# Linear attention and a per-sequence expert on one core: attention output made transposed, its mean square by a matmul with ones, rstd by ln and exp

## The chip, the cores and the metric

The program runs on one core of a Trainium2 chip. The metric is the device time of one execution in microseconds (us); lower is better. The engines are named as the profile names them: PE is TensorE (PEld its weight loads), DVE is VectorE, ACT is ScalarE, POOL is GpSimd and SP is SyncE, which here only issues output transfers.

## The reference

Eight batches, eight heads, 576 positions, head size 64. Attention has no softmax: each head forms a 64 by 64 matrix from k and v, multiplies q by it, and normalises every head's output row by its root mean square. Each batch is then one token for a mixture of experts: the mean over its positions chooses one of eight experts, and the whole batch goes through that expert's two matrices.

```python
def _attn_ref(q, k, v, g_norm):
    kv = np.einsum('bhsd,bhse->bhde', k, v)
    out = np.einsum('bhsd,bhde->bhse', q, kv)
    rms = np.sqrt(np.mean(out * out, axis=-1, keepdims=True) + 1e-06)
    return (out / rms * g_norm).astype(np.float32)
# x: heads side by side, (8, 576, 512)
def _moe_ref(x, w_gate, w1, w2):
    logits = x.mean(axis=1) @ w_gate               # (8 batches, 8 experts)
    e_idx = np.argmax(logits, axis=1)
    ...                                            # gate_w: softmax of the logits at e_idx
    for e in range(E):
        mask = e_idx == e
        h = np.maximum(x[mask] @ w1[e], 0.0)       # 512 -> 1024
        out[mask] = gate_w[mask, None, None] * (h @ w2[e])   # 1024 -> 512
```

All inputs and the output are float32 in HBM. Both kernels turn q, k, v and the expert weights into float16 on the way in, which only POOL's queue does, so all of these loads are issued by POOL.

## The kernel before

A batch is worked in two parts. **Attention** (`emit_attention`) goes over five row blocks (128, 128, 128, 128, 64 positions). q, k, v arrive with positions on partitions: 128 partitions with 4 rows each per head, and a last piece of 64 partitions with one row (L98 and L100: six transfers a batch). ACT rearranges q (L106, L107). PE forms the 64 by 64 matrices head by head, 40 small matmuls a batch (L126), and DVE casts each pair into a block-diagonal tile `kv_dbuf` (L131, L132). For each row block PE transposes q (L211), DVE copies it out (L214), PE makes the output `po` with positions on partitions (L229), ACT squares it (L236), DVE sums the squares per head (L237), ACT copies the output (L240). The reciprocal root is an integer first guess with two Newton steps on DVE (L183 to L196), applied on DVE (L200). One batch later PE transposes the normalised float32 output back (L218) and ACT writes it as `xT` (L222), since the expert needs features on partitions.

**The gate** (`emit_pooled_front`, `emit_pooled_back`) sums the row blocks on DVE (L268 to L271), sums over partitions on POOL with a partition all-reduce (L273), transposes that on PE, multiplies by the gate weights, does a second all-reduce on POOL (L288), then finds the maximum, the index and the softmax value. POOL reads the index (L306) and issues the loads of the chosen expert, `w1f` and `w2f` (L310, L311).

**The expert** of batch b-2 is laid between the steps of batch b's attention: eight units of eight 288-column matmuls into two PSUM tiles `pha`, `phb` (L139, L141) with two Relus on ACT (L143, L144), and five units of eight 512-column matmuls (L152), scaled on DVE (L155) and written by SP (L158). The framework's scheduler orders the instructions on each engine. An engine works its own list strictly in order, so an instruction that waits holds back all that stand behind it, transfers on POOL's list included.

## Time and profile before

| | before |
|---|---|
| median of 3 runs | 307.0 us (305.02 to 308.94) |
| span of the profiled execution | 304.0 us |
| PE busy | 234.4 us (77%) |
| DVE busy | 163.1 us (54%) |
| ACT busy | 128.5 us (42%) |
| POOL busy | 81.9 us (27%) |
| moved by DMA | 40.68 MB, of which 30.94 MB loads by POOL's queue (counted as float16) |
| read from HBM | 61.88 MB |

The profiled execution is one run with its own time, its span; the median of the timed runs lies 3.0 us above it. Busy PE time is counted to the modelled end of each matmul, and matmuls overlap, so the distance between the starts of two matmuls, not the busy time of one, says how fast they follow each other. In the window view the columns are the stretch in us, its length, then for each engine busy us and instructions, then the TensorE clock granted (1.00 is 2.4 GHz, 0.50 is 1.2 GHz), then the DMA share and GB/s.

### The profile page before, as it was taken

To read this page: it belongs to the slowest core of one execution; us is meant where nothing else is said; L and a number is where in the kernel's file an instruction comes from. 1 tells how busy PE (TensorE), PEld (TensorE's weight loads), DVE (VectorE), ACT (ScalarE), POOL (GpSimd) and SP (SyncE) were. 2 spreads that over 40 slices of the span, in tenths; PEclk is the share of its full clock that TensorE was granted. 3 is DMA by queue.
4 is the path that set the end of the run, shared out by engine and by line. 5 is a ranking of instruction groups with operands and counts; after the bars stand their busy time and mean duration, and the time that the engine had idled before them with its cause. 6 is when DMAs were issued, how large, how long until landed. Compare 5 with 4: busy or idle time off the path is not lost.

```text
span 304.0 us, 4581 instructions
## 1 busy us (share of the span) xinstructions
PE 234.4 (77%) x1680; PEld 153.3 (50%) x1680; DVE 163.1 (54%) x532; ACT 128.5 (42%) x273; POOL 81.9 (27%) x88
## 2 busy tenths in 40 slices
PE   0028578716899519997999599989987988599994
PEld 0027456515564317745764377457545744464651
DVE  3004894794038704487749653976495478412122
ACT  1006663704483044942791159136613842440520
POOL 0755415048236123620402040204020420420000
PEclk9999655556799956999999689999997999989999
DMA  0599999079999999999308910595089229839712
GB/s 2 66 174 192 190 192 121 0 82 198 200 185 174 250 201 189 116 166 246 76 0 153 243 38 3 100 233 100 3 151 241 41 20 227 187 59 186 189 59 97
DMA packets 56104, 40.68 MB, mean 134 GB/s; under 512 B 14610, under 2 KB 47378, under 8 KB 56082
## 3 DMA queue, kind: packets, MB, share of 16 engines
q0 software_dynamic: 50176, 30.94, 73.7%
q1 hardware_dynamic: 5906, 9.46, 9.3%
q8 instruction: 13, 0.21, 0.3%
q14 instruction: 9, 0.07, 0.1%
HBM read 61.88 MB, written 9.44 MB: 235 GB/s over the span
## 4 chain that ended last, share of the span: by engine, by line
PE 42%; DMA 35%; DVE 8%; issue 6%; POOL 4%; ACT 3%; POOLq 1%; DVEq 0%; ACTq 0%
DMA w1f<-in_moe_w_dram 13%; PE phb L141 10%; PE pha L139 10%; DMA qb<-in_q_dram 9%; PE pmo L152 8%; PE pkv L126 5%; DMA out_dram<-ot 5%; PE pxt L218 4%; DMA kt<-in_k_dram 4%; DMA vt<-in_v_dram 4%; PE po L229 2%; PE pqt L211 2%; DVE ot L155 1%; POOL zbc L288 1%; POOL pbc L273 1%
## 5 line engine op out<-in xcount | busy, mean ns | idle before, releaser
L152 PE MATMUL pmo<-w2f,hT 128*128 128x512 f16 (+1 forms) x320 | 74.1, 380 | 0.0
L139 PE MATMUL pha<-xT,w1f 128*128 128x288 f16 x256 | 60.1, 303 | 11.9 <-DMA w1f<-in_moe_w_dram 11.6
L141 PE MATMUL phb<-xT,w1f 128*128 128x288 f16 x256 | 59.9, 301 | 1.2 <-ACT hT L143 0.6
L126 PE MATMUL pkv<-vt,kt 128*64 128x64 f16 (+1 forms) x320 | 31.4, 222 | 28.9 <-DMA vt<-in_v_dram 22.7
L273 POOL PARTITION_ALL_REDUCE pbc<-acc x8 | 25.8, 3231 | 87.6 <-DVE acc L271 81.1
L155 DVE TENSOR_SCALAR ot<-pmo,gates_all 128x512 f32<-128x512 f32 (+1 forms) x40 | 29.7, 746 | 34.2 <-PE pmo L152 18.6
L152 PEld LDWEIGHTS <-hT 128*128 128x128 f16 (+1 forms) x320 | 30.3, 100 | 34.5 <-issue 3.4
L143 ACT ACTIVATE hT<-pha 128x288 f16<-128x288 f32 x64 | 27.4, 428 | 42.0 <-PE pha L139 41.8
L126 PEld LDWEIGHTS <-kt 128*64 128x64 f16 (+1 forms) x320 | 23.9, 124 | 38.9 <-issue 17.4
L222 ACT ACTIVATE xT<-pxt,gcol 128x512 f16<-128x512 f32 (+1 forms) x35 | 22.7, 648 | 42.2 <-PE pxt L218 42.1
L139 PEld LDWEIGHTS <-w1f 128*128 128x128 f16 x256 | 26.1, 103 | 21.3 <-DMA w1f<-in_moe_w_dram 12.7
L237 DVE TENSOR_REDUCE ms<-sq_sb 128x8 f32<-128x512 f16 (+1 forms) x40 | 27.2, 681 | 14.4 <-ACT sq_sb L236 13.9
L218 PE MATMUL pxt<-ident,x_sb 128*128 128x128 f32 (+1 forms) x140 | 26.8, 319 | 9.8 <-ACT xT L222 8.1
L236 ACT ACTIVATE sq_sb<-po 128x512 f16<-128x512 f32 (+1 forms) x40 | 24.4, 610 | 22.0 <-PE po L229 21.6
L141 PEld LDWEIGHTS <-w1f 128*128 128x128 f16 x256 | 26.0, 102 | 10.9 <-issue 4.2
L106 ACT COPY qt<-qb 128x2048 f16<-128x2048 f16 x8 | 15.3, 1909 | 36.0 <-DMA qb<-in_q_dram 36.0
L131 DVE CAST kv_dbuf<-pkv 64x64 f16<-64x64 f32 x32 | 6.9, 215 | 42.1 <-PE pkv L126 42.0
L144 ACT ACTIVATE hT<-phb 128x288 f16<-128x288 f32 x64 | 27.0, 421 | 2.9 <-PE phb L141 2.0
L214 DVE COPY qT_sb<-pqt 128x512 f16<-128x512 f16 (+1 forms) x40 | 15.6, 394 | 19.7 <-PE pqt L211 19.2
L200 DVE TENSOR_TENSOR x_sb<-x_sb,y 128x512 f32<-128x512 f32 (+1 forms) x40 | 25.4, 682 | 0.2
L218 PEld LDWEIGHTS pxt<-ident,x_sb 128*128 128x128 f32 (+1 forms) x140 | 18.4, 168 | 12.6 <-ACT xT L222 9.1
L240 ACT COPY x_sb<-po 128x512 f32<-128x512 f32 (+1 forms) x40 | 23.8, 596 | 0.0
(57 smaller groups left out, 225.6 us busy)
## 6 DMA issues: line engine op xcount, KB each, us to landing
w1f<-in_moe_w_dram POOLq DMA_DIRECT2D x8, 1024.0 KB, 9.7
w2f<-in_moe_w_dram POOLq DMA_DIRECT2D x8, 1024.0 KB, 16.4
out_dram<-ot SPq DMA_DIRECT2D x32, 256.0 KB, 6.7
kt<-in_k_dram POOLq DMA_DIRECT2D x8, 512.0 KB, 11.6
vt<-in_v_dram POOLq DMA_DIRECT2D x8, 512.0 KB, 11.9
qb<-in_q_dram POOLq DMA_DIRECT2D x8, 512.0 KB, 12.1
out_dram<-ot SPq DMA_DIRECT2D x8, 128.0 KB, 5.3
kt<-in_k_dram POOLq DMA_DIRECT2D x8, 64.0 KB, 11.1
```

What stands on the lines that cost most here:

```text
L126: nc.tensor.matmul(pkv[o64:o64 + 64, pr, o64:o64 + 64], kt[0:js, h, j, :], vt[0:js, h, j, :], start=(j == 0), stop=(j == NJ - 1),)
L139: nc.tensor.matmul(pha, w1f[:, c, fb * P:(fb + 1) * P], xT[:, b, c, 0:288], start=(c == 0), stop=(c == 3))
L141: nc.tensor.matmul(phb, w1f[:, c, fb * P:(fb + 1) * P], xT[:, b, c, 288:576], start=(c == 0), stop=(c == 3))
L143: nc.scalar.activation(hT[:, fb, 0:288], pha, AF.Relu)
L144: nc.scalar.activation(hT[:, fb, 288:576], phb, AF.Relu)
L152: nc.tensor.matmul(pmo[0:js], hT[:, fc, soff:soff + js], w2f[:, fc, :], start=(fc == 0), stop=(fc == 7))
L155: nc.vector.tensor_scalar(out=ot[0:js], in0=pmo[0:js], scalar1=gates_all[0:js, b:b + 1], scalar2=None, op0=ALU.mult)
L200: nc.vector.tensor_tensor(x_sb[0:js, j, :].rearrange("p (h e) -> p h e", h=H), x_sb[0:js, j, :].rearrange("p (h e) -> p h e", h=H), y0[0:j ...
L218: nc.tensor.transpose(pxt[:, c, 0:js], xo_sb[0:js, i, c * P:(c + 1) * P], ident[0:js, 0:js])
L236: nc.scalar.activation(sq_sb[0:js], po[0:js], AF.Square)
L237: nc.vector.reduce_sum(ms[0:js, j, :], sq_sb[0:js].rearrange("p (h e) -> p h e", h=H), axis=AX.X)
L273: nc.gpsimd.partition_all_reduce(pbc, acc, P, ReduceOp.add)
```

## The change

The change rewrites the whole kernel around another layout:

- **Loads.** A head's 576 positions are loaded as 96 partitions with 6 rows each: one transfer for each of k, v, q of a batch instead of two, 768 instead of 1536 pieces. Batch 0 is split in two halves of four heads. Three pool buffers for the expert weights instead of two.
- **Relayout.** DVE rearranges q and k (`s_re`, L98); ACT did it for q before.
- **Attention transposed.** PE transposes q per head pair (L107), forms two heads' matrices in one 128-column matmul (L118, 24 a batch instead of 40), and makes the output with features on partitions (L129), 288 columns at a time. The transposition back (L218 before) is gone.
- **Mean square.** ACT squares (L132); a matmul with a block-diagonal matrix of 1/64 (L145) sums over the 64 features of each head and spreads the sum over them; ACT takes Ln and Exp with scale -0.5 (L148, L150). One DVE instruction multiplies by the root and by g, writes `xT` in float16 and sums over the positions on the way (L151).
- **Gate.** Four small float32 matmuls on that sum (L159) give the logits on all partitions; the two all-reduces on POOL are gone.
- **Expert.** Relu over 576 columns in one instruction (L214), the scaling over two blocks at once (L231). Rows of the output leave as pieces of 32, 64 or 96 partitions (L241, nine transfers a batch instead of five).
- **Order.** The order is that of the Python code, per engine. Batches 0 and 1 do their attention alone; then the expert of batch b carries the attention of batch b+2 between its 13 units. Two PSUM groups, `a` and `m`, of two double banks each.

```diff
+    for b in (0, 1):
+        for u in att_steps(b, ("a", "m")):
+            u()
+    for b in range(B):
+        mu = moe_units(b)                      # m_1 x8, m_2 x5
+        au = att_steps(b + 2, ("a",)) if b + 2 < B else []
+        first = 1
+        ai = 0
+        for i, u in enumerate(mu):
+            u()
+            want = 0 if i < first else -(-len(au) * (i - first + 1) // (len(mu) - first))
+            while ai < want:
+                au[ai]()
+                ai += 1
...
+    def s_re(b, hs):
+        for n, i in (("qr", 2), ("kr", 0)):
+            nc.vector.tensor_copy(s[n][0:R, :, hs, :],
+                                  kvq[b][i][0:R, hs].rearrange("p h j d -> p j h d"))
...
+    def s_m(b, c, tag):
+        for i in range(2):
+            nc.tensor.matmul(pm[:, i, 0:HS], ones, sq[:, i * HS:(i + 1) * HS],
+                             start=True, stop=True)
+        nc.scalar.activation(ln.rearrange("p (i n) -> p i n", i=2), pm[:, :, 0:HS],
+                             AF.Ln, bias=epsc)
+        nc.scalar.activation(ln, ln, AF.Exp, scale=-0.5)
+        nc.vector.scalar_tensor_tensor(out=s["xT"][:, c, :], in0=o, scalar=gcol, in1=ln,
+                                       op0=ALU.mult, op1=ALU.mult,
+                                       accum_out=s["pl"][:, c:c + 1])
...
+    def s_gate(b, tag):
+        for c in range(NP):
+            nc.tensor.matmul(pg, s["pl"][:, c:c + 1].to_broadcast([P, P]), wg[:, c, :],
+                             start=(c == 0), stop=(c == NP - 1))
...
+        ev = nc.gpsimd.value_load(ix[0:1, 0:1], min_val=0, max_val=E - 1)
...
+        nc.gpsimd.dma_start(w1, moe_w1[ds(ev, 1)].rearrange("o (c p) f -> p (o c) f", p=P))
+        nc.gpsimd.dma_start(w2, moe_w2[ds(ev, 1)].rearrange("o (c p) d -> p (o c) d", p=P))
+        if b + 2 < B:
+            load_qkv(b + 2, 1)
-        pbc = att.tile([P, D], F32, tag="pbc")
-        nc.gpsimd.partition_all_reduce(pbc, acc, P, ReduceOp.add)
...
-        nc.gpsimd.partition_all_reduce(zbc, zt, P, ReduceOp.add)
...
-                pxt = psT.tile([P, 4, P], F32, tag="t")
-                for c in range(4):
-                    nc.tensor.transpose(pxt[:, c, 0:js],
-                                        xo_sb[0:js, i, c * P:(c + 1) * P],
-                                        ident[0:js, 0:js])
```

**POOL's list at the start of the program.** `ident` is the identity matrix for the transposes, `kt`, `vt`, `qb` or `qt` are the loads of k, v, q. First before, then after:

```order
masks.py:197 MEMSET ident 128x128
masks.py:197 MEMSET ident_96 128x128
masks.py:199 ISA
masks.py:199 AFFINE_SELECT ident<-ident 128x128
masks.py:199 AFFINE_SELECT ident_96<-ident_96 128x128
L98 DMA kt<-in_k_dram 128x8x256
L100 DMA kt<-in_k_dram 64x8x64
L98 DMA vt<-in_v_dram 128x8x256
L100 DMA vt<-in_v_dram 64x8x64
```

```order
L64 DMA kt<-in_k_dram 96x4x384
L64 DMA vt<-in_v_dram 96x4x384
L64 DMA qt<-in_q_dram 96x4x384
L64 DMA kt<-in_k_dram 96x4x384
L64 DMA vt<-in_v_dram 96x4x384
L64 DMA qt<-in_q_dram 96x4x384
masks.py:197 MEMSET ident 128x128
masks.py:199 ISA
masks.py:199 AFFINE_SELECT ident<-ident 128x128
```

The six loads of batch 0 now stand ahead of the making of the identity.

**POOL's list around an expert load in the middle of the program** (before: batch 1's expert; `pbc` and `zbc` are the two all-reduces, `ix` the chosen index), first before, then after:

```order
L273 ISA pbc<-acc 128x512
L100 DMA vt<-in_v_dram 64x8x64
L98 DMA qb<-in_q_dram 128x8x256
L100 DMA qb<-in_q_dram 64x8x64
L98 DMA kt<-in_k_dram 128x8x256
L100 DMA kt<-in_k_dram 64x8x64
L98 DMA vt<-in_v_dram 128x8x256
L288 ISA zbc<-zt 128x32
L100 DMA vt<-in_v_dram 64x8x64
L306 TENSOR_LOAD ix_897
L306 ISA x2
L310 DMA w1f<-in_moe_w_dram 128x4x1024
```

```order
L172 TENSOR_LOAD ix
L172 ISA x2
L175 ISA
L175 DMA w_423<-in_moe_w_dram 128x4x1024
L176 ISA
L176 DMA w_424<-in_moe_w_dram 128x8x512
L64 DMA kt<-in_k_dram 96x8x384
L64 DMA vt<-in_v_dram 96x8x384
L64 DMA qt<-in_q_dram 96x8x384
```

The only instruction on POOL that waits for DVE's work is now the read of the index; five transfers stand right behind it, the expert of batch b first and then q, k, v of batch b+2.

**DVE's list after the change, from the end of one round to the start of the next** (`ot` is an expert's output, `lg` to `gates` the gate of batch b+2, then the relayout of batch b+3, whose q and k must have landed):

```order
L151 SCALAR_TENSOR_TENSOR xT,pl<-o,gcol,ln 128x576
L231 TENSOR_SCALAR ot<-ps_m,gates 64x512
L162 COPY lg<-ps_a 128x8
L165 MAX mx<-lg 128x8
L166 MAX_INDEX ix<-mx,lg 128x8
L167 TENSOR_SCALAR lg<-lg,mx 128x8
L171 RECIPROCAL gates<-gs 128x1
L98 COPY qr<-qt 96x3072
L98 COPY kr<-kt 96x3072
L109 COPY qT<-ps_a 128x576 x4
```

None of these stood so before: there the relayout was ACT's, and the gate lay in the middle of a later batch's attention.

## Rows read from the trace of the kernel before

**Rows 1.** Page: span, and PE's busy time, share and instructions.

```profile
span 304.0 us, 4581 instructions
PE 234.4 (77%) x1680; PEld 153.3 (50%) x1680; DVE 163.1 (54%) x532; ACT 128.5 (42%) x273; POOL 81.9 (27%) x88
```

**Rows 2.** Windows by stage: stretch, length, engines' busy us, granted clock, DMA share, GB/s.

```profile
52.00:62.00 10.00, 7.23 (x60) 5.42 (x58) 6.57 (x32) 6.75 (x11) 0.01 (x1) 0.50 0.01 2
192.20:221.00 28.80, 26.59 (x212) 16.92 (x211) 19.42 (x66) 13.64 (x32) 5.41 (x4) 1.00 0.58 115
221.00:247.40 26.40, 23.07 (x163) 15.37 (x163) 16.86 (x55) 13.42 (x32) 5.40 (x4) 0.94 0.64 125
```

**Rows 3.** Waits: engine, line, for whom, us in total, times, longest.

```profile
POOL pbc L273 <- DVE acc L271: 81.1, 7, 15.6
...
PE pkv L126 <- DMA vt<-in_v_dram: 22.7, 3, 19.8
```

**Rows 4.** Timeline of the start: start us, us, engine, line, operation, idle before.

```profile
9.17 0.54 POOL masks.py:199 TENSOR_SCALAR_AFFINE_SELECT ident<-ident 128x128 f32<-128x128 f32 x2 [7.97 <-issue]
9.66 1.20 POOL L98 DMA_DIRECT2D kt<-in_k_dram  x1
...
22.82 1.90 ACT L106 COPY qt<-qb 128x2048 f16<-128x2048 f16 x1 [20.68 <-DMA qb<-in_q_dram]
```

**Rows 5.** Windows while only q, k, v load, and while an expert loads and outputs leave.

```profile
30.00:40.00 10.00, 6.27 (x64) 4.76 (x62) 8.17 (x35) 5.97 (x11) 4.85 (x7) 0.66 1.58 192
193.50:209.00 15.50, 14.06 (x116) 8.96 (x114) 13.03 (x37) 5.51 (x12) 0.76 (x2) 1.00 1.04 200
```

**Rows 6.** Chain that ended last, at the lower clock: start us, us, what.

```profile
57.96 1.12 PE pkv L126 x10
```

**Rows 7.** Timeline of PE at the full clock (starts tell the pace).

```profile
204.36 0.84 PE L126 MATMUL pkv<-vt,kt 128*64 128x64 f16 x10
205.13 0.40 PE L211 MATMUL pqt<-ident,qt 128*128 128x128 f16 x4
205.37 0.61 PE L218 MATMUL pxt<-ident,x_sb 128*128 128x128 f32 x4
...
272.71 8.91 PE L152 MATMUL pmo<-w2f,hT 128*128 128x512 f16 x40
...
283.52 0.28 PE L139 MATMUL pha<-xT,w1f 128*128 128x288 f16 x1
283.64 0.29 PE L141 MATMUL phb<-xT,w1f 128*128 128x288 f16 x1
...
284.67 0.28 PE L139 MATMUL pha<-xT,w1f 128*128 128x288 f16 x1
```

**Rows 8.** Groups by form: line, engine, operation, shapes, count, busy us, mean ns, idle before.

```profile
L143 ACT ACTIVATE hT<-pha 128x288 f16<-128x288 f32 x64 | 27.4, 428 | 42.0 <-PE pha L139 41.8
...
L155 DVE TENSOR_SCALAR ot<-pmo,gates_all 128x512 f32<-128x512 f32 x32 | 23.7, 747 | 23.3 <-PE pmo L152 17.5 <-PE phb L141 4.4 <-DMA out_dram<-ot 1.2
...
L200 DVE TENSOR_TENSOR x_sb<-x_sb,y 128x512 f32<-128x512 f32 x32 | 19.9, 683 | 0.0
L236 ACT ACTIVATE sq_sb<-po 128x512 f16<-128x512 f32 x32 | 19.7, 615 | 8.5 <-PE po L229 8.0 <-DVE ms L237 0.4
...
L214 DVE COPY qT_sb<-pqt 128x512 f16<-128x512 f16 x32 | 13.3, 421 | 10.2 <-PE pqt L211 9.7
...
L304 PEld LDWEIGHTS pg<-gsum,ones_row 1*128 1x128 f32 x16 | 2.5, 198 | 11.5 <-issue 7.0 <-DVE gsum L302 2.4 <-PE pmo L152 1.9
...
L214 DVE COPY qT_sb<-pqt 128x256 f16<-128x256 f16 x8 | 2.3, 288 | 9.5 <-PE pqt L211 9.4
```

**Rows 9.** Timeline around an expert load, and at the end: start us, us, engine, line.

```profile
190.77 0.15 DVE L295 FIND_INDEX8 ix<-mx,lrow 1x8 uint32<-1x8 f32 x1
...
192.22 0.76 POOL L310 DMA_DIRECT2D w1f<-in_moe_w_dram  x1 [1.99 <-DVE ot L155]
...
299.61 0.74 DVE L155 TENSOR_SCALAR ot<-pmo,gates_all 64x512 f32<-64x512 f32 x1 [1.09 <-PE pmo L152]
```

More of the change, by code (lines that the diff above doesn't have):

```diff
@@ new lines, in m_1 @@
+    def m_1(b, fb):
+        s = st[b]
+        if fb == 0:
+            s["hT"] = hp.tile([P, 8, S], F16, tag="hT", name="hT")
+        w1 = s["w"][0]
+        ph = psum("m")
+        for c in range(4):
+            for i in range(2):
+                nc.tensor.matmul(ph[:, i, 0:HS], w1[:, c, fb * P:(fb + 1) * P],
+                                 s["xT"][:, c, i * HS:(i + 1) * HS],
+                                 start=(c == 0), stop=(c == 3))
+        nc.scalar.activation(s["hT"][:, fb, :].rearrange("p (i n) -> p i n", i=2),
+                             ph[:, :, 0:HS], AF.Relu)
@@ new lines, in moe_units @@
+    def moe_units(b):
+        return ([lambda f=f: m_1(b, f) for f in range(8)]
+                + [lambda t=t: m_2(b, t) for t in range(5)])
+    for b in (0, 1):
[12 more added lines that the diff above has]
+                ai += 1
```

418 lines of the change are left out of this document (143 added, 275 removed).

## Prediction

> **What bounds the kernel now.** The page's first part comes first: no engine is full, and PE is the busiest with 234.4 of 304.0 us [rows 1]. So the end is set by PE's work plus what PE waits for, and the windows by stage say where it waits. Early there is a stretch, 52 to 62 us, in which nothing loads (DMA share 0.01) and PE works at a granted clock of 0.50, its lower level of 1.2 GHz; late, from one expert load to the next, a round takes 26.4 to 28.8 us with PE busy 87 to 92% of it at 0.94 to 1.00 [rows 2]. The waits say why loads stop: POOL stood 81.1 us in front of its all-reduce for DVE's sum, and the loads of q, k, v stand behind it on the same list; PE waited 22.7 us for v [rows 3]. The start shows a third cost: 7.97 us in which POOL, making the identity, has issued no load. The first one goes at 9.66 us, and q of batch 0 has landed at 22.82 [rows 4].
>
> How fast loads can be is in two windows. With q, k, v alone 192 GB/s arrive (float16; HBM is read at twice that); with an expert and outputs 200 GB/s together over 15.5 us, which is about what the expert of one round and the outputs beside it need [rows 5]. One batch of q, k, v is 1.77 MB, 9.2 us at 192 GB/s; one expert 2.10 MB. A round of loads is then 15.5 + 9.2 = 24.7 us.
>
> **The parts of the change, and the sum.** I lay the new order out in time, because nearly every instruction moves. Matmul prices are distances between starts.
>
> *Start.* The six loads of batch 0 now go ahead of the identity. The first is issued at about 0.9 us, so the data have landed by 0.9 + (22.82 − 9.66) = 14.1 us. Six issues of some 0.9 us and then the 7.97 us gap put the identity, which the first transpose needs, at 14.8 us. If the gap belongs to POOL's first work of any kind, nothing is gained: bounds 14.8 and 22.8. I take 14.8, since the gap ends in the identity's making and not in a load.
>
> *Attention alone, twice.* Batches 0 and 1 run with nothing beside them, so latencies add. Relayout of q: one DVE copy of 3072 float16 per partition. The rows have no such copy inside SBUF; the nearest is the transposes' copy, 288 ns for 256 and 421 ns for 512, so 0.52 ns each and 1.75 us for 3072; a float32 product at 683 ns for 512 would give about 3.4 us [rows 8]. I take 1.75. Transposes and the k-v matmuls, 48 at the lower clock, 0.11 us each by ten in 1.12 [rows 6]: 5.3. Two casts of 256 columns from PSUM at about 0.45 each (747 ns is the price of 512): 0.9. First output matmuls: 0.7. Then ACT is the chain: 4 Square, 4 Ln, 4 Exp over 576 columns. 428 ns for 288 and 615 for 512 give 0.67; with waits 0.69: 8.3. The last DVE product: 0.75. The gate is four float32 matmuls; before, one float32 product is two passes with loads of 198 ns [rows 8], so eight passes, 1.5. Sum 19.1 us. For batch 0 the relayout is already over at 14.8, so its gate is through PE at 14.8 + 17.4 = 32.2; batch 1's follows after 1.2 us more of gate on DVE: 52.5. I write 52 us to the first expert matmul.
>
> *First round.* The expert of batch 0 is issued 1.45 us after its index was found, as at 190.77 and 192.22 [rows 9]: at 34.5 us. It and q, k, v of batch 2 are 3.87 MB, 20.2 us at 192 GB/s, landed at 56.5. Relayout: 58.3. PE has done its first two expert units (1.9 us each at the lower clock) by 56 and waits 2.3 us. With these units and the next ones at the lower clock the first round is 6 us longer than the rest.
>
> *A round.* PE at the full clock: 64 expert matmuls of 288 columns at 0.12 us (283.52 to 283.64) make 7.7. Before, a unit took 1.15 us instead of 0.96 (283.52 to 284.67), since `phb` waits for a Relu in a rotation of three tiles; now two double tiles rotate, and a Relu of 0.67 us ends within the next unit. Were the gap to stay, 9.2. 40 matmuls of 512 columns: 8.75 (8.91 less the last one's tail). 24 transposes at 0.06 (205.13 to 205.37): 1.45. 24 k-v matmuls at 0.077 (204.36 to 205.13): 1.85. 16 matmuls of output and mean square at 0.12: 1.95 [rows 7]. Gate 1.45. Together 23.15 us.
>
> To this come three waits in PE's own order. (1) The first transpose follows two expert units (1.9 us) after the gate, but DVE must first end the gate (1.7) and copy q (1.75): 1.5 us. What waits behind DVE's copies are the transposes' copies; the expert's PSUM copies come 12 us later. (2) The output matmuls stand right behind the k-v matmuls and wait for both casts: 1.25 us. (3) The gate waits for the last Ln, Exp and product, 2 × 0.69 + 0.75 + some 0.4 of latency, less the one expert unit of 1.73 us beside them: 0.8 us. Round: 23.15 + 3.55 = 26.7 us. DVE has some 18 us in it (two relayouts 3.5, ten copies and casts from PSUM of 0.45 to 0.85, four products of 0.85, output scaling 3.6, gate 1.5) and ACT 13.7 (eight Relus of 0.67 and the 8.3 above), so neither is the bound. The nine outputs on SP and five loads on POOL wait for nothing that PE then waits for.
>
> The loads of a round (24.7 us) are issued some 4.7 us after the round before it ended, and are wanted 30 us after: with 1.5 us of latency they land at 30.9. That is a tie, hidden as long as the rate holds, because q, k, v may queue behind the previous round's.
>
> *Sum.* 52 + 6 + 6 × 26.7 (160.2) + two experts without attention at 7.7 + 8.75 + 0.25 (33.4) + the end as before, 304.0 less the last matmul at some 299.5 (4.5) [rows 1, 9] = 256 us of span. The profiled execution's span was 304.0 us against a median of 307.0, so 3 us are added: **259 us**.
>
> A page's price for the relayout: the Trainium skill, "VectorE: DVE Perf Modes", section "The perf-mode tier table", gives a float16 copy within SBUF four elements a cycle (693 ns for 2048), by which, as an estimate, 3072 would take about 0.95 us and the sum would be some 6 us lower. No row of before shows such a copy.
>
> **A rule against the change.** Before, transfers over 128 partitions bring q, k, v at 192 GB/s [rows 5]; no row shows 96 partitions. If the rate went with the partitions, it would be 144 GB/s and a batch 12.3 us: a round of loads becomes 27.8 us, above PE's 26.7. In favour of the change, a piece is now 6 rows long instead of 4 or 1, and there are half as many. The Trainium skill, "DMA: Bandwidth & Descriptors", section "Rules for kernel authors", asks for 128 partitions and at least 1 MiB a transfer for the most bandwidth, and these have 96 and 0.56 MiB; its section on why a DMA increments its semaphore by 16 says that 96 partitions still use all 16 engines. The first would give the load-bound rival below, the second leaves the sum.
>
> **The rivals.**
> *Loads bound the rounds.* At 27.8 us plus some lost between gate and issue, 28 a round: +1.3 × 6, and +3 in the first round's wait, so 270 us. For it: the tie above. Against it: the DMA share is 1.04 to 1.58 only while loading, and nothing ahead of a load waits any more.
> *Everything a little shorter.* Relayout at under 1 us (−6) and ACT's chain in the lonely attentions overlapping better (16 us each, −6): 247 us.
> *Waits between engines are longer than counted.* Each round crosses from PE to ACT or DVE and back about ten times; 0.33 us more at each is 30 us a round: 259 + 6 × 3.3 + 3 = 282 us. Before, rounds of 26.4 to 28.8 us held more crossings and as much PE work [rows 2].
> *Slower: TensorE stays at its lower level.* If the waits in the rounds kept the clock at 0.50, the 23.15 us of matmuls would become 46: 52 + 6 + 6 × 49.7 + 66 + 4.5 + 3 = 430 us. It decides from where the rounds reach 36 us, that is with the lower clock for 40% of the matmul time: then 313 us. For it: between 52 and 62 us the clock was 0.50 with PE busy 72%. Against it: 0.94 with PE 87% busy [rows 2]; the new rounds have PE at 23.15 of 26.7 us, 87%.
> *The change doesn't do what it says.* Order and lists do stand as described; one table set covers Square, Ln, Exp and Relu in ACT's list, which holds a single table load. No time hangs on this.
>
> **How the numbers follow.** My forecast (251 to 267): 0.48. Shorter throughout (238 to 251): 0.20. Loads bound (267 to 274): 0.16. Longer waits (274 to 300): 0.08. Lower clock (over 313): 0.05; something between 300 and 313: 0.03. The range reaches from 240 to 282, which leaves some 0.04 below and 0.12 above. Faster by over 2% (about what a measurement of this kernel can tell from no change) is below 301 us: 0.91; same 0.03; slower 0.06.
>
> **What would show it.** The first load issued near 1 us and the first transpose near 15; the first expert matmul near 52; expert loads 26 to 28 us apart with PE over 80% busy at a clock near 1.00; q landing about when DVE asks for it; relayout copies near 1.75 us; no POOL wait but for the index. Wrong would be: rounds over 30 us, DVE waiting microseconds for q in every round (loads bound), or a granted clock of 0.50 in the rounds.

## Result and profile after

| | before | after |
|---|---|---|
| median of runs side by side | 306.7 us (305.0 to 308.9, 4 runs) | 247.9 us (246.8 to 251.0, 4 runs) |
| span of the profiled execution | 304.0 us | 245.2 us |

The ratio is 0.807 (95% interval 0.802 to 0.812). The forecast was 259 us, in a range of 240 to 282. The time lies inside the range, 11 us under the figure, in the case called "everything a little shorter".

The page of the kernel after, first part (busy us, share of the span, instructions) and, from the second, the granted clock in 40 slices, in tenths:

```profile
span 245.2 us, 3595 instructions
PE 195.4 (80%) x1408; PEld 128.3 (52%) x1408; DVE 117.7 (48%) x240; ACT 107.9 (44%) x177; POOL 37.8 (15%) x49
...
PEclk9999755555999999988999999999999999999999
```

PE has 39 us less work than in [rows 1] and is still the busiest. Its idle time fell from 69.6 to 49.8 us. The lower clock (digits 5 and 7, some 25 to 60 us) lies in the stretch in which two batches do their attention with nothing beside them, and in the first round; by the pace of the matmuls it begins earlier (last section).

The expert loads on POOL's list cut both programs into three stretches. First two rows of the timeline of before, then of after (start us, us, engine, line, operation, idle before):

```profile
67.66 0.75 POOL L310 DMA_DIRECT2D w1f<-in_moe_w_dram  x1 [2.73 <-DVE tl L194]
...
269.31 0.76 POOL L310 DMA_DIRECT2D w1f<-in_moe_w_dram  x1 [1.98 <-PE pha L139]
```

```profile
1.44 0.81 POOL L64 DMA_DIRECT2D kt<-in_k_dram  x1 [0.87 <-POOLq L277]
...
5.84 0.29 POOL masks.py:199 TENSOR_SCALAR_AFFINE_SELECT ident<-ident 128x128 f16<-128x128 f16 x1
...
32.49 1.31 POOL L175 DMA_DIRECT2D w<-in_moe_w_dram  x1 [23.94 <-DVE gates L171]
...
209.12 0.75 POOL L175 DMA_DIRECT2D w<-in_moe_w_dram  x1 [22.03 <-PE ps_m L211]
```

Up to the first expert load: 67.66 against 32.49, 35.2 us gained. From the first to the last: 201.65 against 176.63, 25.0 us gained over seven loads. From the last to the end: 34.7 against 36.1, 1.4 us lost. Together 58.8, the whole difference of the spans. So three fifths of the gain are in the start, up to the issue of the first expert's load.

One round of after, by the windows from the first expert matmul of a batch to that of the next (columns as in [rows 2]): the first round, three of the five that follow it, and the last two experts, which have no attention beside them.

```profile
48.60:80.40 31.80, 26.50 (x177) 16.82 (x178) 14.20 (x29) 13.47 (x22) 3.94 (x5) 0.80 1.06 180
80.40:104.60 24.20, 22.46 (x179) 14.87 (x179) 14.36 (x30) 13.36 (x22) 4.48 (x5) 1.00 1.05 188
104.60:132.10 27.50, 23.53 (x176) 15.40 (x175) 14.47 (x30) 13.36 (x22) 4.82 (x5) 0.94 1.11 201
...
156.40:182.00 25.60, 22.27 (x176) 14.67 (x176) 14.80 (x30) 13.36 (x22) 4.65 (x5) 1.00 1.17 212
...
206.80:240.30 33.50, 33.44 (x209) 20.06 (x206) 6.99 (x13) 10.59 (x18) 1.64 (x2) 1.00 0.61 133
```

A round that nothing disturbs is 24.2 us with PE busy 22.5; two later ones are 1.4 and 3.3 us longer. The last two experts, 33.5 us, are PE without a pause. PE's own waits in the undisturbed one and in the one behind it are in its timeline:

```profile
82.98 0.43 PE L107 MATMUL ps_a<-ident,qr 96*128 96x96 f16 x6 [0.46 <-DVE qr L98]
...
90.40 0.42 PE L129 MATMUL ps_a<-qT,kvb 128*128 128x288 f16 x2 [0.95 <-DVE kvb L123]
...
99.51 0.40 PE L145 MATMUL ps_a<-sq,ones 128*128 128x288 f16 x2 [0.32 <-DVE o L134]
...
103.66 1.06 PE L159 MATMUL ps_a<-wg,pl 128*128 128x8 f32 x8
...
109.39 0.66 PE L107 MATMUL ps_a<-ident,qr 96*128 96x96 f16 x6 [2.69 <-DVE qr L98]
```

22.5 of work and 0.46 + 0.95 + 0.32 of waits are the 24.2 us. In the round behind it the relayout came 2.2 us later. DVE's rows and the waits (engine, for whom, us in all, times, longest) say why:

```profile
55.61 0.96 DVE L98 COPY qr<-qt 96x3072 f16<-96x3072 f16 x1 [5.39 <-DMA qt<-in_q_dram]
...
108.37 0.96 DVE L98 COPY qr<-qt 96x3072 f16<-96x3072 f16 x1 [2.13 <-DMA qt<-in_q_dram]
```

```profile
DVE qr L98 <- DMA qt<-in_q_dram: 16.6, 5, 5.4
```

Three of these five waits are in the rounds (5.4, 2.1 and 1.3 us); the other two are the landing of batch 0.

### The profile page after: what moved, and what is told of

Read it like the earlier page. It is cut to its first block, busy times and chain, and to the rows that moved or that the text cites. A ratio compares the mean times of both kernels' runs of the same rounds, so it can differ in the third digit from the quotient of the medians.

```text
span 245.2 us, 3595 instructions
## 1 busy us (share of the span) xinstructions
PE 195.4 (80%) x1408; PEld 128.3 (52%) x1408; DVE 117.7 (48%) x240; ACT 107.9 (44%) x177; POOL 37.8 (15%) x49
## 4 chain that ended last, share of the span: by engine, by line
PE 38%; DMA 31%; DVE 10%; ACT 6%; issue 6%; POOL 5%; POOLq 1%; SPq 0%; DVEq 0%
DMA qt<-in_q_dram 29%; PE ps_m L211 17%; PE ps_m L225 11%; DVE ot L231 3%; ACT ln L148 3%; ACT ln L150 3%; PE ps_a L107 3%; PE ps_a L118 2%; DVE qr L98 2%; PE ps_a L145 2%; DMA out_dram<-ot 2%; POOL kt L64 1%; POOL vt L64 1%; DVE xT L151 1%; PE ps_a L129 1%
## 5 line engine op out<-in xcount | busy, mean ns | idle before, releaser
L211 PE MATMUL ps_m<-xT,w 128*128 128x288 f16 x512 | 74.8, 298 | 0.0
L225 PE MATMUL ps_m<-w,hT 128*128 128x512 f16 (+1 forms) x320 | 74.7, 380 | 0.0
L214 ACT ACTIVATE hT<-ps_m 128x576 f16<-128x576 f32 x64 | 41.5, 648 | 47.7 <-PE ps_m L211 46.6
L211 PEld LDWEIGHTS <-w 128*128 128x128 f16 x512 | 50.8, 103 | 13.8 <-issue 0.4
L225 PEld LDWEIGHTS <-hT 128*128 128x128 f16 (+1 forms) x320 | 31.4, 100 | 32.7 <-issue 2.3
L231 DVE TENSOR_SCALAR ot<-ps_m,gates 128x1024 f32<-128x1024 f32 (+1 forms) x24 | 26.4, 1101 | 26.0 <-PE ps_m L225 23.3
L151 DVE SCALAR_TENSOR_TENSOR xT<-o,gcol,ln 128x576 f16<-128x576 f32 x32 | 26.2, 819 | 25.1 <-ACT ln L150 25.1
L132 ACT ACTIVATE sq<-ps_a 128x576 f16<-128x576 f32 x28 | 17.5, 647 | 41.5 <-PE ps_a L129 41.5
L107 PEld LDWEIGHTS <-qr 96*128 96x128 f16 x192 | 12.9, 113 | 30.6 <-DVE qr L98 29.4
L134 DVE COPY o<-ps_a 128x576 f32<-128x576 f32 x28 | 20.6, 753 | 14.6 <-ACT sq L132 14.6
L148 ACT ACTIVATE ln<-ps_a,epsc 128x576 f32<-128x576 f32 x28 | 20.7, 739 | 14.0 <-PE ps_a L145 14.0
L150 ACT ACTIVATE ln<-ln 128x576 f32<-128x576 f32 x32 | 21.8, 683 | 1.0
L107 PE MATMUL ps_a<-ident,qr 96*128 96x96 f16 x168 | 13.9, 227 | 10.3 <-DVE qr L98 10.3
L129 PE MATMUL ps_a<-qT,kvb 128*128 128x288 f16 x56 | 11.6, 309 | 7.6 <-DVE kvb L123 7.6
L145 PE MATMUL ps_a<-sq,ones 128*128 128x288 f16 x56 | 12.1, 300 | 6.3 <-ACT sq L132 4.4
L107 PE MATMUL ps_m<-ident,qr 96*128 96x96 f16 x24 | 2.7, 279 | 16.7 <-DVE qr L98 16.7
L98 DVE COPY qr<-qt 96x3072 f16<-96x3072 f16 (+1 forms) x9 | 7.9, 880 | 16.7 <-DMA qt<-in_q_dram 16.6
L145 PEld LDWEIGHTS <-ones 128*128 128x128 f16 x64 | 6.6, 104 | 14.6 <-issue 10.1
L118 PEld LDWEIGHTS <-kr 96*128 96x128 f16 x192 | 13.7, 111 | 0.3
L159 PE MATMUL ps_a<-wg,pl 128*128 128x8 f32 x64 | 10.4, 279 | 3.8 <-DVE xT L151 3.7
```

The source lines that it names most:

```text
L107: nc.tensor.transpose(pt[:, 0, j * R:(j + 1) * R], s["qr"][0:R, j, 2 * c:2 * c + 2, :], ident[0:R, 0:R])
L118: nc.tensor.matmul(pk[:, c, :], kr[0:R, j, 2 * c:2 * c + 2, :], vt[0:R, 2 * c:2 * c + 2, j, :], start=(j == 0), stop=(j == NJ - 1))
L132: nc.scalar.activation(sq.rearrange("p (i n) -> p i n", i=2), po[:, :, 0:HS], AF.Square)
L134: nc.vector.tensor_copy(o.rearrange("p (i n) -> p i n", i=2), po[:, :, 0:HS])
L145: nc.tensor.matmul(pm[:, i, 0:HS], ones, sq[:, i * HS:(i + 1) * HS], start=True, stop=True)
L148: nc.scalar.activation(ln.rearrange("p (i n) -> p i n", i=2), pm[:, :, 0:HS], AF.Ln, bias=epsc)
```

## Experiments

Times are medians; where nothing else is said, a step is compared with the kernel it was made from.

**The gap ahead of the first load.**

```diff
+    ident = const.tile([P, P], F16)
+    make_identity(nc, ident)
     load_qkv(0, 2)
...
-    ident = const.tile([P, P], F16)
-    make_identity(nc, ident)
```

> The changed kernel with one edit: the identity is made on POOL ahead of the six loads of batch 0, as in the kernel before. In the changed kernel the identity was ready at 6.1 us and no gap of 7.97 us stood anywhere on POOL's list; in the kernel before that gap stood in the identity's making. Theory 1 (the prediction's bound: the gap comes with POOL's first work of that kind, the loads only went past it): the first load is issued near 9.7 us instead of 1.4, everything behind is some 8 us later, the span goes from 245.2 to about 253. Theory 2 (the gap belongs to something else that the kernel before had on POOL's list, its all-reduces' code say, and is gone with it): the identity takes about 0.6 us, the first load goes near 2.1 us, and the span stays within 1 us of 245.2.

Measured: 248.1 us, no change. The last step of the identity took 0.29 us, as in the changed kernel; POOL's timeline at the start of this kernel:

```profile
1.15 0.29 POOL masks.py:199 TENSOR_SCALAR_AFFINE_SELECT ident<-ident 128x128 f16<-128x128 f16 x1
1.63 0.82 POOL L64 DMA_DIRECT2D kt<-in_k_dram  x1 [0.20 <-issue]
```

Theory 2. The gap of [rows 4] is neither the identity's nor that of POOL's first work. What it belongs to, the next run shows from the other side.

**POOL's all-reduces alone.** The kernel before, its two all-reduces made on PE:

```diff
-        nc.gpsimd.partition_all_reduce(pbc, acc, P, ReduceOp.add)
...
-            nc.tensor.transpose(pmis[:, c:c + 1], pbc[0:1, c * P:(c + 1) * P],
-                                ident[0:1, 0:1])
+            nc.tensor.matmul(pmis[:, c:c + 1], pbc[:, c * P:(c + 1) * P],
+                             ones_row[:, 0:1], start=True, stop=True)
...
-        nc.gpsimd.partition_all_reduce(zbc, zt, P, ReduceOp.add)
+        for c in range(4):
+            nc.tensor.matmul(plg[:, 0:E], pooledT[:, c:c + 1].to_broadcast([P, P]),
+                             wg_sb[:, c, :], start=(c == 0), stop=(c == 3))
```

> The kernel before with one edit: the two all-reduces on POOL are replaced by small float32 matmuls with ones and with the gate weights on PE, so that POOL's list holds no wait for DVE's sums any more, only the read of the index. Layout, matmuls and the scheduler's ordering stay as before. From the first expert load (67.7 us before, 32.5 after) to the last (269.3 and 209.1) the changed kernel gains 35 us at the start and 25 us in the rounds. Theory 1 (POOL's list was most of it: loads stood behind the all-reduces, 81.1 us of waits there and 22.7 us of PE waiting for v): the first expert load is issued near 45 us, the stretch without loads between 52 and 62 us is gone, and the time falls by 25 to 35 us, to some 275 us. Theory 2 (the waits on POOL were mostly covered, and the gain is the layout's shorter chain on PE, DVE and ACT): the time falls by under 8 us, rounds stay at 26 to 29 us. If the 7.97 us gap ahead of the first load goes with the all-reduces, 8 us of the gain show at the first load.

Measured: 290.9 us, ratio to before 0.955 (0.946 to 0.965): 14 us, between the two theories. POOL's timeline of this kernel, first load of k, first and last expert load:

```profile
1.25 0.53 POOL masks.py:199 TENSOR_SCALAR_AFFINE_SELECT ident<-ident 128x128 f32<-128x128 f32 x2
1.77 1.01 POOL L98 DMA_DIRECT2D kt<-in_k_dram  x1
...
54.06 0.75 POOL L306 DMA_DIRECT2D w1f<-in_moe_w_dram  x1 [13.10 <-DVE tl L193]
...
256.38 0.76 POOL L306 DMA_DIRECT2D w1f<-in_moe_w_dram  x1 [21.31 <-PE phb L141]
```

With the all-reduces gone the same float32 identity is made without a gap and the first load is issued at 1.8 instead of 9.7 us. The gap goes with the all-reduces being in the program, although the first of them runs much later. (The Trainium skill, "GPSIMD Engine Reference", section "Instruction dispatch", says that the first call to a freshly loaded kernel on these cores pays about 6 us of code loading which the profile does not show as an instruction; the gap here was 7.97 us and stood ahead of another instruction.) That the gap is this code loading, no run here shows. The first expert load moved by 13.6 us: 7.9 of them are the gap; the other 5.7 fit the loads that no longer stand behind an all-reduce, but were not taken apart. From first to last expert load it is 202.3 us against 201.65 before, no gain. The windows of this stretch, before and here:

```profile
67.66:269.31 201.65, 172.41 (x1248) 111.76 (x1248) 120.04 (x391) 96.11 (x215) 53.79 (x49) 0.91 0.84 142
54.06:256.38 202.32, 183.25 (x1354) 122.86 (x1355) 126.26 (x410) 98.33 (x218) 26.27 (x34) 0.93 0.78 135
```

This does not show that POOL's 81.1 us of waits [rows 3] were covered completely. The edit puts float32 passes on PE in place of the all-reduces (17.7 us over the whole program, against 3.6 for the transposes that they replace), and PE is busy 10.8 us longer in a stretch of the same length: its idle time fell from 29.2 to 19.1 us. What the freed list gave in the rounds, if anything, may have been taken up by the new work on PE; the two were not tested apart. As a swap, with what it costs on PE, the edit was worth 14 us, all at the start. The remaining 21.6 us of the start, and all 25.0 of the rounds, do not come with it.

**Loads one round earlier.**

```diff
     load_qkv(1, 1)
+    load_qkv(2, 1)
...
-        if b + 2 < B:
-            load_qkv(b + 2, 1)
+        if b + 3 < B:
+            load_qkv(b + 3, 1)
```

> The changed kernel with q, k, v loaded one round earlier: those of batch 2 are issued at the start behind batch 1's, and the gate step of batch b issues those of batch b+3 (three buffers each are there already). In the changed kernel DVE waited 16.6 us for q in all, 5.4 of them in the first round, and q's landing ended the wait in the rounds of 27.3 and 25.5 us, where the granted clock fell to 0.94. Theory 1 (a tie of latency, as the prediction put it: the rate suffices, the loads only start late): no round waits for q, all take some 24.3 us, the first some 26; the span falls by 6 to 9 us, to some 237. Theory 2 (the loads' rate is the bound: 3.87 MB a round at some 200 GB/s take 19.5 us, more while outputs leave): the wait moves from q to the expert's weights and the span falls by under 3 us. One cost of the edit by either theory: batch 2's loads ahead of the first expert's may delay the first expert matmul from 48.6 us by up to some 3 us.

Measured: 235.0 us (234.9 to 235.4), 12.9 less than the changed kernel. Windows of the first two rounds of this kernel:

```profile
48.80:73.90 25.10, 23.82 (x177) 15.59 (x178) 14.45 (x29) 13.48 (x22) 4.29 (x5) 0.93 1.25 213
73.90:98.10 24.20, 22.47 (x179) 14.88 (x179) 14.35 (x30) 13.37 (x22) 4.42 (x5) 1.00 1.11 204
```

Theory 1, and more of it than expected. The first round fell by 6.7 us, the others that had waited for q went to 24.2, and the first expert matmul stayed at 48.8. In the first round the gain is more than PE's wait of 4.0 us: both kernels begin it at the lower clock, but without the wait PE is at the full one from some 52 us on, with it only from some 61 us (granted over the round: 0.93 and 0.80). Here a wait cost its length and what the clock took around it.

**The order given up to the scheduler.**

```diff
-    ctx.enter_context(tc.manual_schedule())
```

> The changed kernel with the order of the code given up: the framework's scheduler orders the instructions on each engine, as it did in the kernel before. Nothing else is edited. Theory 1 (the shorter time is the layout's, with the freed list on POOL: 64 fewer instructions' worth of waits, no transposition back, no Newton steps): the time stays within 5 us of 248. Theory 2 (the order of the code is a cause of its own: expert units laid between the attention's steps keep PE at work while ACT and DVE answer): the time rises by 10 us or more, with waits of PE for DVE and ACT, and longer rounds.

Measured: 232.6 us (232.1 to 233.1). Neither theory: I had given the scheduler no chance of being faster, and it is by 15.3 us. Its first expert load on POOL, and a window of one of its rounds:

```profile
38.23 1.29 POOL L174 DMA_DIRECT2D w<-in_moe_w_dram  x1 [15.13 <-DVE lg L166]
```

```profile
129.90:152.00 22.10, 21.97 (x177) 14.64 (x175) 14.39 (x29) 12.98 (x23) 1.63 (x3) 1.00 0.83 175
```

PE is at work without a pause; its rounds are 2 us shorter than the undisturbed ones of the changed kernel. The scheduler sets loads as early as a buffer is free, and lays expert units between every step and the copy it needs. It pays for that in its first round: DVE stands 6.9 us in front of a k that comes late, an output copy stands behind that on DVE's list, and PE waits for the copy.

```profile
DVE kr L97 <- DMA kt<-in_k_dram: 11.9, 4, 6.9
...
PE ps_a L144 <- DVE o L133: 7.2, 1, 7.2
```

So the order of the code, as the change has it, is a loss beside the scheduler's. But most of the 15.3 us is the place of the loads: beside the kernel with loads one round earlier (235.0 us), which issues k of batch 2 at 9.4 us as the scheduler does, only 2.4 us are left, or 1%. At the start the order of the code is the better one, by 5.7 us up to the first expert load (32.5 against 38.2).

The layout with its loads carries the gain. The kernel before without its all-reduces (290.9 us) is ordered by the scheduler too, and this one is 58 us faster; its first expert load goes 15.8 us earlier (54.06 there). These 15.8 and the 5.7 of the order are the 21.6 us of the start that were left open above. Which part of the layout gives how much was not taken apart.

**A better order by hand.** The kernel with earlier loads; steps of a round in a new order and at set places; batch 1's relayout and first transposes laid into batch 0's attention.

```diff
-        for c in (0, 2):
-            u.append(lambda c=c: s_o(b, c, tag()))
-            u.append(lambda c=c: s_o(b, c + 1, tag()))
-            u.append(lambda c=c: s_m(b, c, tag()))
-            u.append(lambda c=c: s_m(b, c + 1, tag()))
+        for f, c in ((s_o, 0), (s_o, 1), (s_m, 0), (s_o, 2), (s_m, 1), (s_o, 3),
+                     (s_m, 2), (s_m, 3)):
+            u.append(lambda f=f, c=c: f(b, c, tag()))
...
+    for u in u0[:13] + u1[:1] + u0[13:15] + u1[1:3] + u0[15:] + u1[3:]:
+        u()
+    slots = {0: [0], 2: [1], 3: [2, 3], 4: [4, 5], 6: [6], 7: [7], 8: [8], 9: [9, 10],
+             10: [11, 12], 11: [13], 12: [14]}
```

> The kernel with loads one round earlier, with its order written anew by hand: the output and mean-square steps as o0, o1, m0, o2, m1, o3, m2, m3; one or two expert units between any step and the step that needs its copy; batch 1's relayout and first transposes laid into the first attention. In the kernel with earlier loads a round took 24.2 us, of which PE was busy 22.5: it waited 0.95 us for the casts behind the k-v matmuls, 0.45 for the relayout, 0.3 for an output copy. Theory 1 (PE's work with these waits is all of a round): rounds of 22.3 to 22.8 us, six of them 9 us less, and the first expert matmul some 3 us earlier than 48.8: about 223 us. Theory 2 (a round is held by the chain from its gate to the loads, or by their rate: 4.84 MB a round at some 205 GB/s are 23.6 us): rounds stay above 23.5 us, and the time above 230.

Measured: 221.05 us (220.6 to 221.3), ratio to before 0.722 (0.719 to 0.726): the fastest kernel of the study with the reference's output, 27 us under the changed one. Its first expert matmul starts at 45.56 us. A window of one of its rounds:

```profile
69.50:91.80 22.30, 22.22 (x178) 14.93 (x179) 14.27 (x30) 13.25 (x22) 4.62 (x5) 1.00 1.22 230
```

Theory 1. A round is now PE's work. It also settles the rate: 230 GB/s over 22.3 us are 5.1 MB, which is a whole round's loads and outputs (3.87 + 1.18 MB), and no round waits for them.

**The same order with late loads.** As the kernel just shown, but with the loads where the changed kernel has them.

```diff
-    load_qkv(2, 1)
...
-        if b + 3 < B:
-            load_qkv(b + 3, 1)
+        if b + 2 < B:
+            load_qkv(b + 2, 1)
```

> The hand-ordered kernel with q, k, v loaded where the changed kernel loads them: those of batch b+2 at the gate of batch b. With the two other combinations known (old order and late loads 247.9 us, old order and early loads 235.0, new order and early loads 221.1) this is the fourth. Theory 1 (q's landing, some 21 us after its issue and 26 us after a round's start, sets the rounds as soon as PE needs less): rounds stay at 24 to 27 us, with waits of DVE for q in most of them; of the order's 14 us at most 6 are left, the time is 240 us or more. Theory 2 (the order's gain is PE's own and stands apart from the loads): 13 us are kept, about 234 us.

Measured: 243.8 us (242.5 to 244.6). DVE's timeline:

```profile
108.56 0.96 DVE L98 COPY qr<-qt 96x3072 f16<-96x3072 f16 x1 [5.93 <-DMA qt<-in_q_dram]
132.42 0.94 DVE L98 COPY qr<-qt 96x3072 f16<-96x3072 f16 x1
160.31 0.96 DVE L98 COPY qr<-qt 96x3072 f16<-96x3072 f16 x1 [5.53 <-DMA qt<-in_q_dram]
```

Windows of a round that does not wait and of the next, which does:

```profile
78.90:101.30 22.40, 22.32 (x179) 15.01 (x177) 14.37 (x31) 13.26 (x22) 4.48 (x5) 1.00 1.04 188
101.30:131.20 29.90, 24.41 (x179) 16.12 (x177) 14.39 (x30) 13.25 (x22) 3.97 (x5) 0.89 1.08 199
```

Theory 1. The order is worth some 4 us with late loads, no more than the changed kernel's own runs lie apart, and 14 with early ones; a faster round only waits longer for q. The waits come in every other round, in the changed kernel too: a round that has waited ends later, so that the next q, issued meanwhile, is there in time. From expert load to expert load two rounds together take 52.3 and 51.4 us here, 52.1 and 49.8 in the changed kernel, though a round that does not wait is 1.8 us shorter here (22.4 against 24.2).

**Half of the second expert product left out**, once with the old order and early loads, once with the new order:

```diff
-        for fc in range(8):
+        for fc in range(4):
             nc.tensor.matmul(po[0:n, t % 2, :], s["hT"][:, fc, t * P:t * P + n], w2[:, fc, :],
-                             start=(fc == 0), stop=(fc == 7))
+                             start=(fc == 0), stop=(fc == 3))
```

> The kernel with loads one round earlier, with half of the second expert product left out (four of eight matmuls for each block of the output; the output is then not the reference's). PE's work falls by 20 matmuls of 512 columns, 4.4 us a round; loads, outputs, and the work of ACT and DVE stay. Theory 1 (PE's own work and its waits set a round): rounds fall from 24.2 to about 20 us, and the eight experts together take 35 us less. Theory 2 (the prediction's tie: a round's loads and outputs need 24.7 us): rounds stay at 24 us or above while loads last, DVE waits for q or PE for the weights, and only the two experts without attention at the end get shorter, by 9 us.

Measured: 227.5 and 236.8 us in two runs; the second is the profiled one. A round of it, old order, and rows of PE ahead of it and at its start:

```profile
74.70:99.90 25.20, 21.82 (x158) 14.72 (x158) 14.79 (x30) 13.25 (x22) 4.42 (x5) 0.85 1.08 198
```

```profile
69.77 0.41 PE L146 MATMUL ps_a<-sq,ones 128*128 128x288 f16 x2 [2.17 <-DVE o L135]
...
74.51 0.39 PE L160 MATMUL ps_a<-wg,pl 128*128 128x8 f32 x2 [1.49 <-DVE xT L152]
74.76 3.70 PE L212 MATMUL ps_m<-xT,w 128*128 128x288 f16 x16
```

Neither theory. PE has 4.4 us less to do, and in the profiled run, the longer one, the round is not shorter than 24.2. It isn't the loads: no round waits for q. The shorter units no longer cover the way over ACT and DVE, so PE waits 2.2 us for an output copy and 1.5 at the gate, and then works at the lower clock: the sixteen expert matmuls behind the gate take 3.70 us, against 2.12 in a round at the full clock. The rounds of the shorter run are not on record; it gains only 7.5 us, less than the two last experts alone should give (2 × 4.4), so by this estimate its rounds are no shorter either.

> The hand-ordered kernel with half of the second expert product left out (four of eight matmuls for each block of the output; the output is then not the reference's). With the old order this made the rounds longer, 25 to 26 us instead of 24.2: PE waited 2.2 us for an output copy and 1.5 us at the gate, and after these waits the granted clock was at its lower level. Theory 1 (the waits between engines hold the round and pull the clock down with them; the new order has fewer): rounds of 18 to 21 us at a clock near 1.00. Theory 2 (the same happens here, since half-length units cover the way over ACT and DVE less): rounds above 22 us, with a granted clock under 0.95. Theory 3 (the loads): PE or DVE wait for w or q; a round's 5.05 MB at the 230 GB/s seen in the hand-ordered rounds are 22 us while loads last.

Measured: 213.7 us. Windows of two rounds, new order:

```profile
69.20:90.60 21.40, 18.41 (x158) 12.99 (x158) 14.24 (x30) 13.03 (x22) 4.66 (x5) 1.00 1.22 231
90.60:113.50 22.90, 19.91 (x158) 13.75 (x158) 14.20 (x30) 13.03 (x22) 4.65 (x5) 0.93 1.22 229
```

Between theories 1 and 2, and not 3. With 4.4 us less work the rounds are some 21.4 and 22.9 us in turn: the waits between engines hold them (0.5, 1.2 and 1.4 us of PE for ACT and DVE), the clock takes 1.5 us more in every other one, and PE and DVE wait for no load in a round. So the way over ACT and DVE holds a round at 21.4 us with this order and these shorter units, when PE has only 18.4 to do: not far under the 22.3 that PE needs with the whole product.

**Loads as 64 partitions with 9 rows.**

```diff
-    R = 96
+    R = 64
...
-    pqkv = ctx.enter_context(tc.tile_pool(name="pqkv", bufs=3))
-    wp = ctx.enter_context(tc.tile_pool(name="wp", bufs=3))
+    pqkv = ctx.enter_context(tc.tile_pool(name="pqkv", bufs=2))
+    wp = ctx.enter_context(tc.tile_pool(name="wp", bufs=2))
```

> The changed kernel with q, k, v loaded as 64 partitions with 9 rows each instead of 96 with 6; pieces are half as long again and a third fewer; for the space, two buffers each for q, k, v and for the weights instead of three. PE has 36 transposes and 36 k-v matmuls a batch instead of 24, about 1.2 us a round more; the relayout copies 4608 elements a partition. What counts is the rate while only q, k, v load, between 10 and 20 us: 203 GB/s with 96 partitions, 192 with 128 (and shorter pieces) in the kernel before. Theory 1 (the rate goes with the partitions, as the rival of the prediction had it): 135 GB/s, the second half of batch 0 lands 5 us later and rounds wait for q. Theory 2 (the rate goes with the pieces' length, or with neither): 200 GB/s or more, and only PE's and DVE's work gets longer, by some 2 us a round.

Measured: 268.6 us (267.9 to 269.2). The stretch in which only q, k, v load, of the changed kernel (96 partitions) and of this one:

```profile
10.00:20.00 10.00, 4.84 (x48) 4.37 (x48) 4.33 (x10) 0.00 (x0) 0.00 (x0) 1.00 1.31 203
10.00:20.00 10.00, 5.67 (x69) 5.46 (x70) 4.54 (x8) 0.00 (x0) 0.00 (x0) 1.00 1.21 207
```

Theory 2 for the rate: 207 GB/s over 64 partitions, 203 over 96, 192 over 128 with shorter pieces [rows 5]. A third fewer partitions did not lower the rate, and the rival of the prediction that rested on it (135 GB/s here) is refuted. The pieces are half as long again, and the two were not tested apart. The time itself rose by 20 us, more than the 2 us a round expected: 36 transposes and 36 k-v matmuls, fewer buffers, and relayout copies of 4608 elements at 2.5 us, 0.55 ns an element, where those of 2304 in the same kernel took 0.82 us, 0.36 ns an element. These were not taken apart further.

**Exp left out.**

```diff
-        nc.scalar.activation(ln, ln, AF.Exp, scale=-0.5)
```

> The kernel with loads one round earlier, with the Exp left out (the product takes ln of the mean square in its place; the output is then not the reference's). Four activations of 0.68 us a batch go from ACT, nothing from PE. Theory 1 (the prediction: in the two attentions that run alone ACT is the chain, in the rounds PE is, and the order of the code already hides ACT there): the first expert matmul comes some 5.4 us earlier, at 43.4 instead of 48.8, rounds stay at 24.2 us, the time falls by 5 to 6 us. Theory 2 (the way through Ln and Exp also holds the rounds, at the gate): each round falls by 0.7 us too, and the time by 10 us. If the first expert's weights, issued near 30 us, have not landed by 43.4, that wait takes part of the gain.

Measured: 226.9 us, 8.1 under the kernel it was made from. First expert matmul and a round:

```profile
43.87 3.81 PE L211 MATMUL ps_m<-xT,w 128*128 128x288 f16 x16
```

```profile
68.60:92.20 23.60, 22.23 (x178) 14.80 (x178) 14.64 (x29) 10.64 (x18) 4.69 (x5) 1.00 1.22 228
```

Mostly theory 1: 4.9 us at the start, where ACT is the chain (5.4 were expected). But each round fell by 0.6 us too, near the 0.7 of theory 2: PE's waits in a round went from 1.7 to 1.4 us, and its busy time from 22.5 to 22.2. The wait that is gone is the one of 0.32 us for an output copy (at 99.51 in the rows of after); why PE's busy time fell was not followed further.

**Filling PE's waits at the start.** On the hand-ordered kernel, batch 2's relayout, transposes and k-v matmuls moved into batch 1's attention:

```diff
+    u2 = att_steps(2, ("a",))
-    for u in u0[:13] + u1[:1] + u0[13:15] + u1[1:3] + u0[15:] + u1[3:]:
+    for u in (u0[:13] + u1[:1] + u0[13:15] + u1[1:3] + u0[15:] + u1[3:10]
+              + u2[:1] + u1[10:12] + u2[1:3] + u1[12:14] + u2[3:6] + u1[14:]):
         u()
```

> The hand-ordered kernel with the relayout, the transposes and the k-v matmuls of batch 2 moved from the first round into the attention of batch 1, where PE waits for ACT and DVE. In the hand-ordered kernel PE waited some 7 us between 35 and 46 us, first expert matmul at 45.6 us, and its first round took 24.1 us. Theory 1 (that work, 24 transposes and 24 k-v matmuls, 4.7 us at the lower clock, fits into PE's waits): the first expert matmul stays near 46 us, the first round falls by 2.9 us or more, and the time to some 218 us. Theory 2 (ACT's chain through the second attention is held back by it, DVE's relayout of 1.9 us above all): the first expert matmul comes 2 to 4 us later and the time stays within 1 us of 221.

Measured: 226.45 us (226.1 to 227.0), 5.4 slower. PE's timeline:

```profile
41.42 1.14 PE L108 MATMUL ps_a<-ident,qr 96*128 96x96 f16 x12 [2.49 <-ACT sq L133]
44.05 0.64 PE L146 MATMUL ps_a<-sq,ones 128*128 128x288 f16 x2 [1.49 <-DVE qT L110]
...
53.00 9.03 PE L210 MATMUL ps_m<-xT,w 128*128 128x288 f16 x56
```

Theory 2, and worse than it. The transposes take their banks from the same group `a` as batch 1's outputs, so each waits for the other's copy. The first expert matmul came 7.4 us later, and the first round got only 2.2 us shorter.

## Why the prediction came out 11 us high

The mechanisms were in the main as described: order, lists, what binds where. Two were not: the gap at the start, and the waits for q. Nearly all sizes were too high.

| step | predicted | measured |
|---|---|---|
| first load issued; batch 0 there | 0.9; 14.1 | 1.44; 14.8 |
| identity ready | 14.8 | 6.1 |
| relayout copy of 3072 | 1.75 | 0.95 |
| ACT's chain in a lonely attention | 8.3 | 8.0 and 8.2 |
| gate of batch 0 and 1 through PE | 32.2, 52.5 | 30.3, 48.7 |
| first expert matmul | 52 | 48.6 |
| first round | 32.7 | 31.8 |
| round: PE's work | 23.15 | 22.5 |
| round: PE's waits | 3.55 | 1.7 |
| round | 26.7 | 24.2, with waits for q 25.3 on average |
| last two experts; end | 33.4; 4.5 | 33.5; 4.9 |
| outside the span | 3 | 2.7 |

**The start, 3.4 us too high.** The step that failed in kind is the one on the gap: I let the 7.97 us of [rows 4] move with the identity, because it stood in the identity's making; it belonged to the all-reduces and vanished. It cost little, since the second half of batch 0 landed at 14.8 us anyway. But the first transposes, foreseen near 15 us, came at 11.1 on the first half, so that half of batch 0's were done by then. Batch 1's relayout was half as long as assumed, and most of the gate's eight passes ran while ACT still worked on the last pair, instead of behind it.

**The first round**, 0.9 us off in its length, was right in kind: q landed at 55.6 (56.5 predicted), PE waited 4.0 us for the relayout (2.3), the first units ran at the lower clock. That its length fits so well is partly luck: it was 7.6 us longer than an undisturbed round (6 predicted), and that round 2.5 us shorter.

**The rounds, 1.4 us each too high on average.** The relayout again is the largest term: 0.96 us for a copy in DVE's rows above. I took 0.52 ns an element from copies out of PSUM [rows 8]; inside SBUF it is 0.31. This made wait (1) 0.46 instead of 1.5 us. (The estimate by the Trainium skill's "VectorE: DVE Perf Modes", section "The perf-mode tier table", had been 0.95 us, and the trace agrees, with 0.94 to 0.96 for a copy alone.) Wait (2), for the casts, was 0.95 (1.25). Wait (3) at the gate did not occur; in its place PE waited 0.32 us for an output copy. The gate took 0.92 us (1.45): its loads of weights ran under the passes before. k-v matmuls came 0.056 us apart, 1.35 in all (1.85): those of 128 columns are not even as dear as the ones of 64 at 0.077 [rows 7].

**The tie was put at nothing, and it was not nothing.** I called it hidden as long as the rate holds; the waits for q, with the clock around them, took 1.1 us a round on average (25.3 against 24.2), and more in the first. The length of a round's loads was near what I had counted (24.7 and 1.5 us): an expert's load issued at 82.82 and the q behind it, landed at 108.37, are 25.5 us apart. q's issue in between:

```profile
86.50 0.80 POOL L64 DMA_DIRECT2D qt<-in_q_dram  x1
```

But the rate of this stretch (199 GB/s) is no bound: the hand-ordered kernel moves a round's 5.1 MB within 22.3 us (230 GB/s). What made q late was its place: issued at the gate, behind 2.1 MB of weights, some 21 us before it lands. Two rounds together took 50 to 52 us in this place with either order, and 48.4 and 44.6 us (old order, new order) with the loads one round earlier.

**The rivals.** "Everything a little shorter" came nearest (247 us), in part by luck: the relayout was under 1 us as it had it, but ACT's chain was not shorter by more than 0.3 us; the gate, the k-v matmuls and PE's waits, which it did not name, gave more than the waits for q took. Load-bound rounds by the number of partitions: refuted by the run with 64. Longer waits between engines: they were half of what was counted. The lower clock: in the changed kernel's first round (0.80, as the prediction had priced it) and one behind a wait for q (0.94), in no other; the runs with half a product show that it is real: with less work for PE in a round the clock fell, and took back a part of what was saved. (In that rival one sum is off: with rounds of 36 us its terms give 315 us, not 313.)

**What was not asked.** I treated the order of the code as part of the change's benefit and never priced the scheduler against it. The scheduler's was better by 15 us, some 13 of them by its earlier loads.

## What to carry to other kernels

Ask of every load where it stands on its queue and what was issued ahead of it, before asking for its rate: moving three loads one round earlier was worth 13 us, more than leaving out the Exp (8). Do not count a wait on an engine's list as a gain before looking whether it is covered and what replaces it: taking 81 us of POOL's waits away gave 14 us, all at the start, and put 14 us of work on PE. Once each engine's work is right, lay something of about 1 us between any step and the step that needs its copy, and compare an order written by hand with the scheduler's before keeping it.

## What was not expected of the hardware

- The 7.97 us gap at the start of POOL's list comes with two all-reduces that run much later; without them the same identity is made at once (1.25 us).
- Loads that cast to float16 ran at 207 GB/s over 64 partitions, 203 over 96 and 192 over 128, in the order of the length of their pieces; partitions and length changed together.
- A relayout copy on DVE that met POOL's issue of loads could become longer, and the issue too. After, from the timeline of DVE and of POOL:

```profile
109.25 1.32 DVE L98 COPY kr<-kt 96x3072 f16<-96x3072 f16 x1
```

```profile
108.39 1.42 POOL L176 DMA_DIRECT2D w<-in_moe_w_dram  x1
```

  Alone they take 0.95 and 0.90 us. The copy of q from 108.37 met the same issue and kept its 0.96 us. (The Trainium skill, "SBUF — State Buffer", section "Who interferes with whom", says that such a copy can share ports with POOL, and that the one that comes second waits for the other's whole instruction; the trace agrees that they hinder each other, and the price here was 0.4 us for this copy and 0.5 for this issue.)
- With less work for PE a round became no shorter in the old order's profiled run, the longer of its two: behind a wait of 2.2 us and one of 1.5 us the granted clock fell to its lower level (0.85 over the round). With the new order it was 1.00 and 0.93 in turn; why one round of two kept the full clock there stays open.
- The granted clock is to be read with the matmuls' pace beside it. Two windows of after, in each of which a lonely attention runs:

```profile
11.00:24.00 13.00, 8.12 (x60) 6.06 (x61) 5.60 (x13) 3.01 (x5) 0.00 (x0) 1.00 1.20 186
31.00:48.00 17.00, 10.56 (x70) 7.88 (x70) 10.66 (x21) 8.04 (x14) 4.49 (x5) 0.50 0.91 148
```

  The rows give 1.00 and 0.50, but the 24 k-v matmuls take 2.76 us in both, and 1.50 in a round at 1.00. By the pace the first is at the lower level too, as the prediction had assumed for both.
